# Stores of eight combined output blocks as tasks of their own, later in the order

## The chip, the cores and the metric

The kernel runs on one core of one Trainium2 chip. The metric is the device time of one execution in microseconds (us). A run has several executions; the time before is a median of three runs.

## The reference

The reference chains three parts: an attention through 32 memory slots per head, a first expert layer, and a second expert layer with four gated experts. Only the last one matters here:

```python
def _moe2_ref(x, domain_probs, w1, w2):
    p = domain_probs / (domain_probs.sum(-1, keepdims=True) + 1e-09)
    out = np.zeros((N, D), dtype=np.float32)        # N = 2304, D = 512
    for e in range(E):                              # E = 4, F = 1024
        h = np.maximum(x @ w1[e], 0.0)
        out += p[:, e:e + 1] * (h @ w2[e])
    return out.astype(np.float32)
```

The kernel writes the output transposed, as 512 rows of 2304 tokens. The tokens are four batches of 576.

## The kernel before, in words

The last layer works on units of one group of 512 hidden columns (eight groups g, two to an expert) and one batch b. Batches 0 and 1 go through all eight groups first (units 00, 01, 10, ... 71, written group then batch), then batches 2 and 3 (units 02, 03, 12, ... 73). Every product of blocks of two by two is done with seven products in place of eight, and each product in three passes of split operands. In a unit, `Up` makes the hidden blocks (product, line 894, six matmuls of 128x288 at line 899) and `Seven` multiplies them by the second weights (product, line 1051, six matmuls at line 1064): 14 products per unit, tasks D02_0 to D02_13 for group 0 and batch 2. The result of D02_n lies in one of two PSUM banks (pool ps_h, two buffers, tiles c020 to c0213) until its task F02_n (flush, line 1072) adds it to an accumulator in SBUF; in group 0 the flush is a copy on ScalarE (line 1082).

The accumulators of a batch are seven blocks of 128x2x288. Four of them (P2, P3, P4, P5) lie in one tile, acc0 for batch 0, and end as the four output blocks. The pool of these tiles has two buffers: acc2 of batch 2 takes the memory of acc0, and acc3 that of acc1. The first flush into acc2 is F02_4 and the first into acc3 is F03_2, both copies on ScalarE. Each must come after the last reader of the old tile.

When batches 0 and 1 are through their eighth group, `combine` (line 1086) turns the seven blocks into the four output blocks, with seven tensor additions per batch, tasks cb00 to cb06 and cb10 to cb16 on VectorE or GpSimd. The additions 1, 4, 5 and 6 complete an output block; right behind each of these, in the same task, SyncE issues the store of 288 KB to the output (line 1097). That is eight stores for batches 0 and 1. Batch 2 is combined at the end of the program and batch 3 is stored by another path.

All tasks stand in one list written out by hand, `ORDER`. Every engine gets its instructions in the order of that list, and so does SyncE, which issues all DMAs. SyncE issues one DMA after the other: where one waits for a semaphore, those behind it wait too. Among the DMAs around the change are loads of the next unit's weights: tasks wr (line 827, into the tiles w170 and w171 in place, piece by piece as TensorE has read the old one) and cl (line 861, into tiles w2c in a ring of seven), reloads of batch 3 (line 733), gates (line 882) and writes of derived weights to DRAM (line 820).

Of the kernel before, what the change touches and what calls it, by code (L numbers as in the profile page):

```python
# [185 lines left out]
c22_021 p1_030 v1_030 D71_10 cl00 cl02 D71_13 x3l1 cl03 F71_13 p4_021 c21_021 F71_10 sk7S1 x3h3 D02_1 H02_1 p3_021
cb06 x3h6 x3l6 p1_031 E71_11 D71_11 x3l3 F71_11 x3t2 cl01 p5_031 F02_1 cb04 D71_12 D02_0 x3t3 x3h5 c12_021 x3h4 x3l4
p5_030 p6_030 wr103 cl06 F02_0 v16_030 p2_030 c11_030 F71_12 p7_030 cb05 x3l5 wr100 v1_031 p6_031 wr113 p2_031 wr105
v167_030 p4_030 c22_030 p3_030 S02_4 H02_4 cb11 H02_2 L02_2 p5_120 D02_4 F02_4 L02_1 c12_030 v16_031 cl04 H02_3 D02_2
c21_030 D02_3 S02_5 L02_4 L02_3 p7_031 cb10 F02_3 F02_2 D02_5 D02_6 p1_120 H03_0 F02_5 v167_031 D02_7 p4_031 cl05  # L190
S02_6 wr102 H02_6 F02_7 wr106 H02_5 wr115 D02_9 F02_9 cb12 cb15 c11_031 c22_031 F02_6 v1_120 p3_031 D02_8 F02_8 L03_0
D03_1 L02_5 D02_11 L02_6 F03_1 D02_13 F02_11 D02_12 wr110 S03_1 c12_031 H03_3 wr112 F02_12 p2_120 H03_1 F02_13 D03_0
c21_031 F03_0 cb13 cb16 L03_1 L03_3 p6_120 v16_120 H03_2 wr116 L03_2 D02_10 F02_10 c11_120 cb14 S03_4 cl10 H03_4 D03_2
L03_4 F03_2 p7_120 v167_120 c22_120 D03_3 F03_3 cl11 D03_4 F03_4 S03_5 H03_5 p4_120 c21_120 H12_0 L03_5 L12_0 D03_5
F03_5 cl12 p3_120 c12_120 D03_6 F03_6 p1_121 v1_121 D03_7 F03_7 cl13 p6_121 v16_121 D03_8 F03_8 S03_6 H03_6 p5_121
p2_121 c11_121 D03_9 F03_9 cl14 p7_121 v167_121 c22_121 D03_10 F03_10 D03_11 F03_11 cl15 S12_1 H12_1 L03_6 p4_121
c21_121 H12_2 L12_2 D03_12 F03_12 L12_1 p3_121 c12_121 D03_13 F03_13 cl16 p1_130 v1_130 D12_0 F12_0 p6_130 H12_3
v16_130 pg12 D12_1 F12_1 S12_4 H12_4 L12_4 L12_3 p5_130 p2_130 c11_130 D12_2 F12_2 wr200 wr203 p7_130 v167_130 c22_130
D12_3 F12_3 D12_4 F12_4 S12_5 H12_5 p4_130 c21_130 H13_0 L12_5 L13_0 wr205 wr202 D12_5 F12_5 p3_130 c12_130 wr206
D12_6 F12_6 p1_131 v1_131 D12_7 F12_7 p6_131 v16_131 D12_8 F12_8 S12_6 H12_6 p5_131 p2_131 c11_131 D12_9 F12_9 wr210  # L200
wr213 p7_131 v167_131 c22_131 D12_10 F12_10 D12_11 F12_11 S13_1 H13_1 L12_6 p4_131 c21_131 H13_2 L13_2 wr215 wr212
D12_12 F12_12 L13_1 p3_131 c12_131 wr216 D12_13 F12_13 p1_220 v1_220 D13_0 F13_0 p6_220 H13_3 v16_220 pg13 D13_1 F13_1
cl20 S13_4 H13_4 L13_4 L13_3 p5_220 p2_220 c11_220 D13_2 F13_2 p7_220 v167_220 c22_220 D13_3 F13_3 cl21 D13_4 F13_4
S13_5 H13_5 p4_220 c21_220 H22_0 L13_5 L22_0 D13_5 F13_5 cl22 p3_220 c12_220 D13_6 F13_6 p1_221 v1_221 D13_7 F13_7
cl23 p6_221 v16_221 D13_8 F13_8 S13_6 H13_6 p5_221 p2_221 c11_221 D13_9 F13_9 cl24 p7_221 v167_221 c22_221 D13_10
F13_10 D13_11 F13_11 cl25 S22_1 H22_1 L13_6 p4_221 c21_221 H22_2 L22_2 D13_12 F13_12 L22_1 p3_221 c12_221 D13_13
F13_13 cl26 p1_230 v1_230 D22_0 F22_0 p6_230 H22_3 v16_230 D22_1 F22_1 S22_4 H22_4 L22_4 L22_3 p5_230 p2_230 c11_230
D22_2 F22_2 wr300 wr303 p7_230 v167_230 c22_230 D22_3 F22_3 D22_4 F22_4 S22_5 H22_5 p4_230 c21_230 H23_0 L22_5 L23_0
wr305 wr302 D22_5 F22_5 p3_230 c12_230 wr306 D22_6 F22_6 p1_231 v1_231 D22_7 F22_7 p6_231 v16_231 D22_8 F22_8 S22_6
H22_6 p5_231 p2_231 c11_231 D22_9 F22_9 wr310 wr313 p7_231 v167_231 c22_231 D22_10 F22_10 D22_11 F22_11 S23_1 H23_1  # L210
L22_6 p4_231 c21_231 H23_2 L23_2 wr315 wr312 D22_12 F22_12 L23_1 p3_231 c12_231 wr316 D22_13 F22_13 p1_320 v1_320
D23_0 F23_0 p6_320 H23_3 v16_320 D23_1 F23_1 cl30 S23_4 H23_4 L23_4 L23_3 p5_320 p2_320 c11_320 D23_2 F23_2 p7_320
v167_320 c22_320 D23_3 F23_3 cl31 D23_4 F23_4 S23_5 H23_5 p4_320 c21_320 H32_0 L23_5 L32_0 D23_5 F23_5 cl32 p3_320
c12_320 D23_6 F23_6 p1_321 v1_321 D23_7 F23_7 cl33 p6_321 v16_321 D23_8 F23_8 S23_6 H23_6 p5_321 p2_321 c11_321 D23_9
F23_9 cl34 p7_321 v167_321 c22_321 D23_10 F23_10 D23_11 F23_11 cl35 S32_1 H32_1 L23_6 p4_321 c21_321 H32_2 L32_2
D23_12 F23_12 L32_1 p3_321 c12_321 D23_13 F23_13 cl36 p1_330 v1_330 D32_0 F32_0 p6_330 H32_3 v16_330 pg22 D32_1 F32_1
S32_4 H32_4 L32_4 L32_3 p5_330 p2_330 c11_330 D32_2 F32_2 wr400 wr403 p7_330 v167_330 c22_330 D32_3 F32_3 D32_4 F32_4
S32_5 H32_5 p4_330 c21_330 H33_0 L32_5 L33_0 wr405 wr402 D32_5 F32_5 p3_330 c12_330 wr406 D32_6 F32_6 p1_331 v1_331
D32_7 F32_7 p6_331 v16_331 D32_8 F32_8 S32_6 H32_6 p5_331 p2_331 c11_331 D32_9 F32_9 wr410 wr413 p7_331 v167_331
c22_331 D32_10 F32_10 D32_11 F32_11 S33_1 H33_1 L32_6 p4_331 c21_331 H33_2 L33_2 wr415 wr412 D32_12 F32_12 L33_1  # L220
p3_331 c12_331 wr416 D32_13 F32_13 p1_420 v1_420 D33_0 F33_0 p6_420 H33_3 v16_420 pg23 D33_1 F33_1 cl40 S33_4 H33_4
L33_4 L33_3 p5_420 p2_420 c11_420 D33_2 F33_2 p7_420 v167_420 c22_420 D33_3 F33_3 cl41 D33_4 F33_4 S33_5 H33_5 p4_420
c21_420 H42_0 L33_5 L42_0 D33_5 F33_5 cl42 p3_420 c12_420 D33_6 F33_6 p1_421 v1_421 D33_7 F33_7 cl43 p6_421 v16_421
D33_8 F33_8 S33_6 H33_6 p5_421 p2_421 c11_421 D33_9 F33_9 cl44 p7_421 v167_421 c22_421 D33_10 F33_10 D33_11 F33_11
cl45 S42_1 H42_1 L33_6 p4_421 c21_421 H42_2 L42_2 D33_12 F33_12 L42_1 p3_421 c12_421 D33_13 F33_13 cl46 p1_430 v1_430
D42_0 F42_0 p6_430 H42_3 v16_430 D42_1 F42_1 S42_4 H42_4 L42_4 L42_3 p5_430 p2_430 c11_430 D42_2 F42_2 wr500 wr503
p7_430 v167_430 c22_430 D42_3 F42_3 D42_4 F42_4 S42_5 H42_5 p4_430 c21_430 H43_0 L42_5 L43_0 wr505 wr502 D42_5 F42_5
p3_430 c12_430 wr506 D42_6 F42_6 p1_431 v1_431 D42_7 F42_7 p6_431 v16_431 D42_8 F42_8 S42_6 H42_6 p5_431 p2_431
c11_431 D42_9 F42_9 wr510 wr513 p7_431 v167_431 c22_431 D42_10 F42_10 D42_11 F42_11 S43_1 H43_1 L42_6 p4_431 c21_431
H43_2 L43_2 wr515 wr512 D42_12 F42_12 L43_1 p3_431 c12_431 wr516 D42_13 F42_13 p1_520 v1_520 D43_0 F43_0 p6_520 H43_3  # L230
v16_520 D43_1 F43_1 cl50 S43_4 H43_4 L43_4 L43_3 p5_520 p2_520 c11_520 D43_2 F43_2 p7_520 v167_520 c22_520 D43_3 F43_3
cl51 D43_4 F43_4 S43_5 H43_5 p4_520 c21_520 H52_0 L43_5 L52_0 D43_5 F43_5 cl52 p3_520 c12_520 D43_6 F43_6 p1_521
v1_521 D43_7 F43_7 cl53 p6_521 v16_521 D43_8 F43_8 S43_6 H43_6 p5_521 p2_521 c11_521 D43_9 F43_9 cl54 p7_521 v167_521
c22_521 D43_10 F43_10 D43_11 F43_11 cl55 S52_1 H52_1 L43_6 p4_521 c21_521 H52_2 L52_2 D43_12 p1_530 L52_1 F43_12
p3_521 c12_521 D43_13 F43_13 cl56 v1_530 D52_0 F52_0 p6_530 v16_530 pg32 H52_3 S52_4 D52_1 F52_1 H52_4 L52_4 p5_530
wr603 p2_530 c11_530 D52_2 wr600 F52_2 p7_530 v167_530 c22_530 D52_3 F52_3 D52_4 S52_5 F52_4 L52_3 p4_530 c21_530
H53_0 L53_0 wr605 H52_5 L52_5 wr602 D52_5 F52_5 p1_531 p3_530 wr606 c12_530 D52_6 F52_6 D52_7 v1_531 p6_531 F52_7
D52_8 F52_8 S52_6 H52_6 L52_6 D52_9 F52_9 p5_531 wr613 v16_531 p2_531 c11_531 p7_531 v167_531 c22_531 D52_10 F52_10
S53_1 H53_1 p4_531 c21_531 H53_2 L53_2 D52_12 F52_12 D52_11 p5_620 wr612 L53_1 p3_531 wr616 p1_620 v1_620 F52_11
# [1348 lines left out]
```

## Time and profile before

| | us |
|---|---|
| median of 3 runs | 1100.35 (1099.81 to 1100.35) |
| the profiled execution | 1100.15 |
| its span, first to last instruction | 1098.4 |
| PE (TensorE matmul) busy | 1089.1 (99% of the span) |
| DVE (VectorE) busy | 804.6 |
| ACT (ScalarE) busy | 562.1 |
| POOL (GpSimd) busy | 548.3 |

The profile names engines by these short names; SP is SyncE and SPq its queue of DMA issues. A bracket [0.92 <-DMA w2c<-kS] behind a row is the time that the engine stood idle before it, and what ended the wait. The granted clock of TensorE is given as a share of its full 2.4 GHz.

### The profile page before, as it was taken

The page shows a single profiled execution, that of the slowest core. Times are in us where ns is not written, and L with a number is a line of the kernel's source. Part 1 is how long each engine was busy: PE and PEld are TensorE (multiplying, and loading weights), DVE is VectorE, ACT ScalarE, POOL GpSimd, SP SyncE. Part 2 cuts the span into 40 slices and gives each one's busy share as a digit, 9 for nine tenths or more (in the row PEclk, how much of TensorE's full clock was granted, in tenths as well). Part 3 has the DMA queues.
Part 4 walks back from the last instruction along what each step waited for, and adds up shares of the span by engine and source line. Part 5 has one row for each costly group of instructions (what it writes and reads, how often), then busy time and mean ns, then how long its engine had stood idle before and what let it go on. Part 6 is the DMA issues. An engine that isn't in the chain of part 4 may idle for free.

```text
span 1098.4 us, 22039 instructions
## 1 busy us (share of the span) xinstructions
PE 1089.1 (99%) x8550; PEld 1055.4 (96%) x8550; DVE 804.6 (73%) x1520; ACT 562.1 (51%) x1236; POOL 548.3 (50%) x443
## 2 busy tenths in 40 slices
...
GB/s 375 395 149 20 81 75 59 77 22 59 1 52 37 154 137 306 198 235 260 203 198 225 252 233 188 266 239 287 192 182 166 163 193 154 176 164 165 184 144 87
DMA packets 62584, 185.40 MB, mean 169 GB/s; under 512 B 6288, under 2 KB 24720, under 8 KB 58768
## 3 DMA queue, kind: packets, MB, share of 16 engines
...
HBM read 117.62 MB, written 66.36 MB: 167 GB/s over the span
## 4 chain that ended last, share of the span: by engine, by line
PE 96%; DVE 2%; DMA 1%; issue 0%; SPq 0%; POOL 0%; ACT 0%; DVEq 0%; POOLq 0%
PE c L1064 30%; PE y L705 18%; PE uy L899 13%; PE uw L899 9%; PE ux L899 9%; PE h L671 9%; PE y L702 1%; PE pw L630 1%; PE warm L337 1%; PE o L1010 1%; PE pm L439 1%; PE h L668 1%; DMA w2c<-kS 1%; DMA w<-kw 1%; PE pc L471 0%; DVE h L1037 0%
## 5 line engine op out<-in xcount | busy, mean ns | idle before, releaser
L324 POOL TENSOR_TENSOR gc<-h,gc 128x576 fp32r<-128x576 f32 x102 | 149.5, 1473 | 204.7 <-ACT gc L1045 204.3
L705 PE MATMUL y<-g,wout 128*128 128x288 f32 x1440 | 205.5, 296 | 0.0
L705 PEld LDWEIGHTS y<-g,wout 128*128 128x128 f32 x1440 | 195.4, 188 | 7.3 <-ACT g L690 2.5
L1045 ACT CAST gc<-h 128x576 fp32r<-128x576 f32 x217 | 142.9, 674 | 115.0 <-DVE h L1037 69.8
L1064 PE MATMUL c<-gc,w2c 128*128 128x288 f32 x1260 | 192.3, 295 | 0.9 <-DMA w2c<-kS 0.9
L1084 DVE TENSOR_TENSOR acc<-c,acc 128x288 f32<-128x288 f32 x280 | 124.2, 453 | 83.5 <-PE c L1064 83.0
L899 PE MATMUL uy<-x,w 128*128 128x288 f32 x1152 | 183.1, 295 | 0.2 <-DMA w<-kw 0.2
L1064 PEld LDWEIGHTS c<-gc,w2c 128*128 128x128 f32 x1260 | 175.3, 188 | 1.3 <-ACT gc L1045 1.1
L899 PEld LDWEIGHTS uy<-x,w 128*128 128x128 f32 x1152 | 163.0, 188 | 0.4 <-ACT v L971 0.4
L324 POOL TENSOR_TENSOR g<-act,g 128x288 fp32r<-128x288 f32 x81 | 70.3, 875 | 123.6 <-ACT g L690 92.6
L899 PE MATMUL uw<-x,w 128*128 128x288 f32 x768 | 122.9, 296 | 0.2
L899 PE MATMUL ux<-x,w 128*128 128x288 f32 x768 | 121.7, 295 | 0.0
L1064 PE MATMUL c<-gc,sS 128*128 128x288 f32 x768 | 117.8, 295 | 1.1 <-DVE acc L1084 1.1
L671 PE MATMUL h<-a,wp 128*128 128x288 f32 x720 | 110.2, 296 | 0.0
L899 PEld LDWEIGHTS uw<-x,w 128*128 128x128 f32 x768 | 108.7, 188 | 0.9 <-DVE ux L936 0.6
L899 PEld LDWEIGHTS ux<-x,w 128*128 128x128 f32 x768 | 108.7, 188 | 0.0
L324 DVE TENSOR_TENSOR gc<-h,gc 128x576 fp32r<-128x576 f32 x115 | 100.5, 883 | 10.9 <-ACT gc L1045 10.7
L1064 PEld LDWEIGHTS c<-gc,sS 128*128 128x128 f32 x768 | 106.9, 188 | 1.4 <-DVE acc L1084 1.4
L686 DVE SCALAR_TENSOR_TENSOR act<-neg,bet,h 128x288 f32<-128x288 f32 x120 | 60.3, 510 | 63.9 <-ACT neg L677 57.4
L671 PEld LDWEIGHTS h<-a,wp 128*128 128x128 f32 x720 | 99.9, 188 | 5.7 <-issue 2.3
L677 ACT ACTIVATE neg<-h 128x288 f32<-128x288 f32 x128 | 52.1, 411 | 98.0 <-PE h L671 95.5
L1082 ACT COPY acc<-c 128x288 f32<-128x288 f32 x154 | 60.3, 401 | 75.1 <-PE c L1064 74.1
...
## 6 DMA issues: line engine op xcount, KB each, us to landing
...
```

What stands on the lines that cost most here:

```text
L324: eng.tensor_tensor(out=out, in0=in0, in1=in1.bitcast(F32), op=ALU.subtract)
L337: mm(p[:, 0:128], ident, ident, start=True, stop=True)
L439: mm(p[32 * h:32 * h + 32, 0:128], l, r, start=(c == 0), stop=(c == 4))
L671: mm(p, wp_t[b, c, g][:, x, fs], a_t[b][:, y, g, o:o + HB], start=(n == 0), stop=(n == 5))
L677: nc.scalar.activation(out=self.neg, in_=self.p, func=AF.Relu, scale=-1.0)
L686: nc.vector.scalar_tensor_tensor(out=self.g, in0=self.neg, scalar=bet[:, ft:ft + 1], in1=self.p, op0=ALU.mult, op1=ALU.add)
L705: mm(First.acc[d], w[:, x, d * 128:(d + 1) * 128], self.gt[:, y, 0:HB], start=(self.start and n == 0), stop=(self.stop and n == 2))
L899: mm(p, w[:, x, a, k], operand(self.b, i)[:, y, k], start=(start and n == 0), stop=(n == 5), skip_group_check=not start)
L1045: nc.scalar.copy(out=t[:, 0], in_=self.raw(q))
L1064: mm(p, w[:, x, i, m * 128:(m + 1) * 128], self.g_t[q][:, y, i], start=(fresh and k == 0), stop=(k == 5), skip_group_check=not fresh)
L1082: nc.scalar.copy(out=a, in_=self.ps[n])
L1084: nc.vector.tensor_tensor(out=a, in0=self.ps[n], in1=a, op=ALU.add)
```

## The change

The store leaves `combine` and becomes a function of its own. For batches 0 and 1 it is a task cs, added to the plan for the additions 1, 4, 5 and 6; in `ORDER` each cs stands some 14 tasks behind its cb. Batch 2 stores as before. Only the eight cs are new in the list; the rest of it is the same, with other line breaks. Of the list the first changed line is shown, where cs01 comes in 14 tasks behind cb01.

```diff
-p1_021 S71_6 E70_13 D71_1 F71_1 E71_5 vl711 pg03 D70_13 cb00 F70_13 x3t0 p5_021 E71_3 D71_5 D71_3 v16_020 F71_5 x2h6
...
+p1_021 S71_6 E70_13 D71_1 F71_1 E71_5 vl711 pg03 D70_13 cb00 F70_13 cs01 x3t0 p5_021 E71_3 D71_5 D71_3 v16_020 F71_5
...
-        if b < 3 and o in (P2, P3, P4, P5):
+        if b == 2:
+            store(b, n)
+
+    def store(b, n):
+
+        o = (P6, P2, P7, P6, P3, P4, P5)[n]
+        a = acc_t[b]
+        if o in (P2, P3, P4, P5):
             i, j = divmod((P2, P3, P4, P5).index(o), 2)
             rows = out[i * 256:(i + 1) * 256, b * S + j * HB:b * S + (j + 1) * HB]
             nc.sync.dma_start(out=rows.rearrange("(m p) n -> p m n", p=128), in_=a[o])
...
         def do_combine(b, n):
             do(f"cb{b}{n}", combine, b, n)
+            if b < 2 and n in (1, 4, 5, 6):
+                do(f"cs{b}{n}", store, b, n)
```

No instruction is added or removed. On the compute engines no instruction changes its place. What moves is on SyncE, in three stretches; two of them follow. In these rows a name like w2c06 is a tile (down weights of group 0, product 6), the number behind it a buffer, and the brackets list the semaphores that the instruction waits for. DMAs take eight semaphores DMAHW0 to DMAHW7 in turn, and each first waits for the DMA that had its semaphore before, so a DMA's own semaphore is among those in its brackets, except where that wait is left out because it holds already.

SyncE from the second store of acc0 to the load of w2c04, before:

```order
L1097 DMA out_0<-acc0_5207 128x2x288 [waits DMAHW4_49,DVE_49]
L861 DMA w2c01_9885<-kS10_5760 128x1024 [waits DMAHW5_49,PE_49]
L1097 DMA out_0<-acc0_5207 128x2x288 [waits DMAHW6_49,DVE_49]
L827 DMA w170_8872<-kw110_5794 128x2x512 [waits DMAHW7_49,PE_49]
L861 DMA w2c06_9936<-kw2011_5830 128x1024 [waits DMAHW3_49,DMAHW0_49]
L1097 DMA out_0<-acc0_5207 128x2x288 [waits DMAHW1_49,DVE_49]
L827 DMA w170_8872<-kw110_5794 128x2x512 [waits DMAHW2_49,PE_49]
L827 DMA w171_8992<-kw111_5895 128x2x512 [waits PE_49]
L827 DMA w170_8872<-kw110_5794 128x2x256 [waits DMAHW4_49]
L1097 DMA out_0<-acc1_5524 128x2x288 [waits DMAHW5_49,Pool_49]
L861 DMA w2c04_10018<-kS30_5751 128x1024 [waits DMAHW6_49]
```

And with the change:

```order
L861 DMA w2c01_9884<-kS10_5760 128x1024 [waits DMAHW4_49,PE_49]
L1104 DMA out_0<-acc0_5207 128x2x288 [waits DMAHW5_49,DVE_49]
L827 DMA w170_8872<-kw110_5794 128x2x512 [waits DMAHW6_49,PE_49]
L861 DMA w2c06_9935<-kw2011_5830 128x1024 [waits DMAHW7_49,DMAHW3_49]
L1104 DMA out_0<-acc0_5207 128x2x288 [waits DMAHW0_49,DVE_49]
L827 DMA w170_8872<-kw110_5794 128x2x512 [waits DMAHW1_49,PE_49]
L827 DMA w171_8992<-kw111_5895 128x2x512 [waits DMAHW2_49,PE_49]
L827 DMA w170_8872<-kw110_5794 128x2x256
L1104 DMA out_0<-acc0_5207 128x2x288 [waits DMAHW4_49,DVE_49]
L861 DMA w2c04_10017<-kS30_5751 128x1024 [waits DMAHW5_49]
L1104 DMA out_0<-acc1_5524 128x2x288 [waits DMAHW6_49,Pool_49]
```

The last store of acc0 stood ahead of the three loads into w170 and w171, and stands behind them now.

SyncE from the third store of acc1 to the load of w2c11 or the last store of acc1, before and with the change:

```order
L1097 DMA out_0<-acc1_5524 128x2x288 [waits DMAHW6_49,DVE_49]
L827 DMA w171_8992<-kw111_5895 128x2x256 [waits DMAHW7_49,PE_49]
L1097 DMA out_0<-acc1_5524 128x2x288 [waits DMAHW0_49,Pool_49]
L861 DMA w2c10_10217<-kw2100_6010 128x1024 [waits DMAHW1_49,PE_49]
L861 DMA w2c11_10247<-kS11_5704 128x1024 [waits DMAHW2_49,PE_49]
```

```order
L827 DMA w171_8992<-kw111_5895 128x2x256 [waits DMAHW6_49,PE_49]
L861 DMA w2c10_10215<-kw2100_6010 128x1024 [waits DMAHW7_49,PE_49]
L1104 DMA out_0<-acc1_5524 128x2x288 [waits DMAHW0_49,DVE_49]
L861 DMA w2c11_10246<-kS11_5704 128x1024 [waits DMAHW1_49,PE_49]
L1104 DMA out_0<-acc1_5524 128x2x288 [waits DMAHW2_49,Pool_49]
```

The last store of acc1 now stands behind the load of w2c11. That load goes into the buffer of w2c01 and waits for TensorE to finish the last product that reads w2c01, which is c033.

Who waits for these stores has not moved. ScalarE around F02_4 (the copy of c024 into acc2), and TensorE at the products behind it, with the change:

```order
L1045 CAST gc0_5140<-h021_9727 128x576
L1082 COPY acc2_9893<-c024_10004 128x288 [waits DMAHW1_49,DMAHW4_49,DMAHW0_49,DMAHW5_49,DVE_49,PE_49]
L945 COPY v16031_10015<-uy031_9959 128x288 [waits DVE_49,Activation_49]
L1045 CAST gc0_5140<-h021_9727 128x576
L1082 COPY acc2_9893<-c023_10028 128x288 [waits PE_49]
```

```order
L1064 MATMUL c024_10004<-gc0_5140,w2c02_9823 128x288 x4
L1064 MATMUL c022_10020<-gc2_5260,w2c01_9884 128x288 [waits DMAHW4_49]
L1064 MATMUL c022_10020<-gc2_5260,w2c01_9884 128x288 [waits DVE_49]
L1064 MATMUL c022_10020<-gc2_5260,w2c01_9884 128x288 x4
L1064 MATMUL c023_10028<-gc2_5260,w2c01_9884 128x288 [waits Activation_49]
```

The copy waits for four DMAs, the four stores of acc0; before they are those on DMAHW7, 4, 6 and 1, with the change those on DMAHW1, 5, 0 and 4, the last of which is the third row from the end of the second list. The wait of c023 on ScalarE is for this copy, since c023 takes the PSUM bank of c024. F03_2 waits in the same way for the four stores of acc1, and c034, two products behind c032, for F03_2.

## Rows read from the trace of the kernel before

**Rows 1.** The page, first part: busy time by engine.

```profile
PE 1089.1 (99%) x8550; PEld 1055.4 (96%) x8550; DVE 804.6 (73%) x1520; ACT 562.1 (51%) x1236; POOL 548.3 (50%) x443
```

**Rows 2.** Waits of PE from 700 to 850 us: total, times, longest.

```profile
PE c L1064 <- DVE acc L1084: 1.1, 1, 1.1
PE c L1064 <- DMA w2c<-kS: 0.9, 1, 0.9
```

**Rows 3.** Waits of SyncE's queue, 715 to 780 us, same columns.

```profile
SPq L1097 <- DVE acc L1093: 21.9, 5, 7.3
...
SPq L1097 <- DVE ux L936: 1.9, 1, 1.9
```

**Rows 4.** Timeline of SyncE around the stores: start, length, DMA issued.

```profile
746.68 0.42 SPq L861 DMA_DIRECT2D w2c<-kS  x1
748.22 0.39 SPq L1097 DMA_DIRECT2D out<-acc  x1
751.88 0.53 SPq L827 DMA_DIRECT2D w<-kw  x1
752.50 0.55 SPq L861 DMA_DIRECT2D w2c<-kw  x1
754.65 0.39 SPq L1097 DMA_DIRECT2D out<-acc  x1
755.15 2.04 SPq L827 DMA_DIRECT2D w<-kw  x3
757.29 0.54 SPq L1097 DMA_DIRECT2D out<-acc  x1
757.88 0.46 SPq L861 DMA_DIRECT2D w2c<-kS  x1
...
771.60 0.38 SPq L1097 DMA_DIRECT2D out<-acc  x1
773.04 0.34 SPq L861 DMA_DIRECT2D w2c<-kw  x1
777.02 0.34 SPq L861 DMA_DIRECT2D w2c<-kS  x1
```

**Rows 5.** Issue to landing, us, of stores issued at 746.20, 748.22, 754.65, 757.29, 771.60.

```profile
out<-acc SPq DMA_DIRECT2D x1, 288.0 KB, 2.4
...
out<-acc SPq DMA_DIRECT2D x1, 288.0 KB, 4.3
...
out<-acc SPq DMA_DIRECT2D x1, 288.0 KB, 3.6
...
out<-acc SPq DMA_DIRECT2D x1, 288.0 KB, 7.0
...
out<-acc SPq DMA_DIRECT2D x1, 288.0 KB, 3.3
```

**Rows 6.** Timeline of PE: products of units 02 and 03.

```profile
757.29 2.67 PE L1064 MATMUL c<-gc,w2c 128*128 128x288 f32 x18
...
765.63 1.03 PE L1064 MATMUL c<-gc,w2c 128*128 128x288 f32 x6 [0.92 <-DMA w2c<-kS]
...
773.65 1.75 PE L1064 MATMUL c<-gc,w2c 128*128 128x288 f32 x12
775.24 0.96 PE L899 MATMUL uy<-x,w 128*128 128x288 f32 x6
776.03 1.75 PE L1064 MATMUL c<-gc,w2c 128*128 128x288 f32 x12
```

**Rows 7.** Timeline of ACT: F02_4 and F03_2.

```profile
758.43 0.40 ACT L1082 COPY acc<-c 128x288 f32<-128x288 f32 x1 [3.41 <-PE c L1064]
...
775.64 0.41 ACT L1082 COPY acc<-c 128x288 f32<-128x288 f32 x1
```

**Rows 8.** Windows: length, busy (count) of PE, clock, DMA share, GB/s (first two); all engines (last two).

```profile
1.36:5.10 3.74, 3.74 (x18) 1.00 0.84 241
5.10:8.84 3.74, 3.74 (x36) 1.00 1.06 409
...
1094.75:1096.90 2.15, 0.00 (x0) 0.00 (x0) 0.46 (x1) 0.00 (x0) 0.00 (x0) 1.00 0.74 255
...
1097.30:1097.40 0.10, 0.00 (x0) 0.00 (x0) 0.00 (x0) 0.00 (x0) 0.00 (x0) 0.50 0.00 0
```

More of the change, by code (lines that the diff above doesn't have):

```diff
@@ L186 @@
[L186 to L239, printed above, removed]
-D52_13 F52_13 wr615 c12_531 D53_0 F53_0 S53_4 H53_3 p6_620 v16_620 wr610 pg33 H53_4 D53_1 F53_1 L53_3 L53_4 S53_5
@@ L241 @@
-p2_620 p7_620 c11_620 D53_2 F53_2 v167_620 c22_620 D53_4 F53_4 D53_3 cl60 F53_3 cl61 p4_620 H53_5 L53_5 c21_620 H62_0
-L62_0 D53_5 F53_5 p3_620 c12_620 D53_6 cl64 p1_621 D53_7 F53_6 v1_621 p6_621 D53_8 F53_8 F53_7 v16_621 S53_6 H53_6
-p2_621 c11_621 D53_9 F53_9 p7_621 cl62 p5_621 v167_621 c22_621 D53_10 F53_10 S62_1 H62_1 D53_11 F53_11 p4_621 p3_621
-c12_621 c21_621 L53_6 H62_2 D53_12 F53_12 p1_630 L62_2 L62_1 D53_13 F53_13 v1_630 D62_0 H62_3 p6_630 v16_630 F62_0
-D62_1 F62_1 p5_630 S62_4 H62_4 L62_3 p2_630 c11_630 D62_2 cl65 F62_2 wr700 wr703 p7_630 D62_4 v167_630 c22_630 D62_3
@@ new lines @@
+x2h6 D71_6 wr012 H71_5 x2l6 wr015 c11_020 us310 x3h2 p7_020 vk711 F71_3 F71_6 x3l2 v1_021 v167_020 p5_020 c22_020
+D70_12 F70_12 D71_8 F71_8 H71_6 p2_021 c11_021 E71_7 x2l5 p4_020 D71_7 c21_020 cb02 F71_7 L71_5 D71_4 F71_4 H02_0
+L71_6 p3_020 us311 E71_9 E71_13 c12_020 cb03 p6_021 v16_021 x3l0 L02_0 S02_1 wr016 D71_9 F71_9 p7_021 x3t1 v167_021
+x3h1 c22_021 p1_030 v1_030 D71_10 cl00 cl02 D71_13 x3l1 cl03 F71_13 p4_021 c21_021 F71_10 sk7S1 x3h3 D02_1 H02_1
+p3_021 cb06 x3h6 x3l6 p1_031 E71_11 D71_11 x3l3 F71_11 x3t2 cl01 p5_031 F02_1 cb04 D71_12 cs06 D02_0 x3t3 x3h5 c12_021
@@ new lines @@
+x3h4 x3l4 p5_030 p6_030 wr103 cl06 F02_0 v16_030 cs04 p2_030 c11_030 F71_12 p7_030 cb05 x3l5 wr100 v1_031 p6_031 wr113
+p2_031 wr105 v167_030 p4_030 c22_030 p3_030 S02_4 H02_4 cs05 cb11 H02_2 L02_2 p5_120 D02_4 F02_4 L02_1 c12_030 v16_031
+cl04 H02_3 D02_2 c21_030 D02_3 cs11 S02_5 L02_4 L02_3 p7_031 cb10 F02_3 F02_2 D02_5 D02_6 p1_120 H03_0 F02_5 v167_031
+D02_7 p4_031 cl05 S02_6 wr102 H02_6 F02_7 wr106 H02_5 wr115 D02_9 F02_9 cb12 cb15 c11_031 c22_031 F02_6 v1_120 p3_031
+D02_8 F02_8 L03_0 D03_1 L02_5 D02_11 L02_6 F03_1 cs15 D02_13 F02_11 D02_12 wr110 S03_1 c12_031 H03_3 wr112 F02_12
@@ new lines @@
+p2_120 H03_1 F02_13 D03_0 c21_031 F03_0 cb13 cb16 L03_1 L03_3 p6_120 v16_120 H03_2 wr116 L03_2 D02_10 F02_10 c11_120
+cb14 S03_4 cl10 cs16 H03_4 D03_2 L03_4 F03_2 p7_120 v167_120 c22_120 D03_3 F03_3 cl11 D03_4 cs14 F03_4 S03_5 H03_5
+p4_120 c21_120 H12_0 L03_5 L12_0 D03_5 F03_5 cl12 p3_120 c12_120 D03_6 F03_6 p1_121 v1_121 D03_7 F03_7 cl13 p6_121
+v16_121 D03_8 F03_8 S03_6 H03_6 p5_121 p2_121 c11_121 D03_9 F03_9 cl14 p7_121 v167_121 c22_121 D03_10 F03_10 D03_11
+F03_11 cl15 S12_1 H12_1 L03_6 p4_121 c21_121 H12_2 L12_2 D03_12 F03_12 L12_1 p3_121 c12_121 D03_13 F03_13 cl16 p1_130
@@ new lines @@
+v1_130 D12_0 F12_0 p6_130 H12_3 v16_130 pg12 D12_1 F12_1 S12_4 H12_4 L12_4 L12_3 p5_130 p2_130 c11_130 D12_2 F12_2
+wr200 wr203 p7_130 v167_130 c22_130 D12_3 F12_3 D12_4 F12_4 S12_5 H12_5 p4_130 c21_130 H13_0 L12_5 L13_0 wr205 wr202
+D12_5 F12_5 p3_130 c12_130 wr206 D12_6 F12_6 p1_131 v1_131 D12_7 F12_7 p6_131 v16_131 D12_8 F12_8 S12_6 H12_6 p5_131
+p2_131 c11_131 D12_9 F12_9 wr210 wr213 p7_131 v167_131 c22_131 D12_10 F12_10 D12_11 F12_11 S13_1 H13_1 L12_6 p4_131
+c21_131 H13_2 L13_2 wr215 wr212 D12_12 F12_12 L13_1 p3_131 c12_131 wr216 D12_13 F12_13 p1_220 v1_220 D13_0 F13_0
@@ new lines @@
+p6_220 H13_3 v16_220 pg13 D13_1 F13_1 cl20 S13_4 H13_4 L13_4 L13_3 p5_220 p2_220 c11_220 D13_2 F13_2 p7_220 v167_220
+c22_220 D13_3 F13_3 cl21 D13_4 F13_4 S13_5 H13_5 p4_220 c21_220 H22_0 L13_5 L22_0 D13_5 F13_5 cl22 p3_220 c12_220
+D13_6 F13_6 p1_221 v1_221 D13_7 F13_7 cl23 p6_221 v16_221 D13_8 F13_8 S13_6 H13_6 p5_221 p2_221 c11_221 D13_9 F13_9
+cl24 p7_221 v167_221 c22_221 D13_10 F13_10 D13_11 F13_11 cl25 S22_1 H22_1 L13_6 p4_221 c21_221 H22_2 L22_2 D13_12
+F13_12 L22_1 p3_221 c12_221 D13_13 F13_13 cl26 p1_230 v1_230 D22_0 F22_0 p6_230 H22_3 v16_230 D22_1 F22_1 S22_4 H22_4
@@ new lines @@
+L22_4 L22_3 p5_230 p2_230 c11_230 D22_2 F22_2 wr300 wr303 p7_230 v167_230 c22_230 D22_3 F22_3 D22_4 F22_4 S22_5 H22_5
+p4_230 c21_230 H23_0 L22_5 L23_0 wr305 wr302 D22_5 F22_5 p3_230 c12_230 wr306 D22_6 F22_6 p1_231 v1_231 D22_7 F22_7
+p6_231 v16_231 D22_8 F22_8 S22_6 H22_6 p5_231 p2_231 c11_231 D22_9 F22_9 wr310 wr313 p7_231 v167_231 c22_231 D22_10
+F22_10 D22_11 F22_11 S23_1 H23_1 L22_6 p4_231 c21_231 H23_2 L23_2 wr315 wr312 D22_12 F22_12 L23_1 p3_231 c12_231 wr316
+D22_13 F22_13 p1_320 v1_320 D23_0 F23_0 p6_320 H23_3 v16_320 D23_1 F23_1 cl30 S23_4 H23_4 L23_4 L23_3 p5_320 p2_320
@@ new lines @@
+c11_320 D23_2 F23_2 p7_320 v167_320 c22_320 D23_3 F23_3 cl31 D23_4 F23_4 S23_5 H23_5 p4_320 c21_320 H32_0 L23_5 L32_0
+D23_5 F23_5 cl32 p3_320 c12_320 D23_6 F23_6 p1_321 v1_321 D23_7 F23_7 cl33 p6_321 v16_321 D23_8 F23_8 S23_6 H23_6
+p5_321 p2_321 c11_321 D23_9 F23_9 cl34 p7_321 v167_321 c22_321 D23_10 F23_10 D23_11 F23_11 cl35 S32_1 H32_1 L23_6
+p4_321 c21_321 H32_2 L32_2 D23_12 F23_12 L32_1 p3_321 c12_321 D23_13 F23_13 cl36 p1_330 v1_330 D32_0 F32_0 p6_330
+H32_3 v16_330 pg22 D32_1 F32_1 S32_4 H32_4 L32_4 L32_3 p5_330 p2_330 c11_330 D32_2 F32_2 wr400 wr403 p7_330 v167_330
@@ new lines @@
+c22_330 D32_3 F32_3 D32_4 F32_4 S32_5 H32_5 p4_330 c21_330 H33_0 L32_5 L33_0 wr405 wr402 D32_5 F32_5 p3_330 c12_330
+wr406 D32_6 F32_6 p1_331 v1_331 D32_7 F32_7 p6_331 v16_331 D32_8 F32_8 S32_6 H32_6 p5_331 p2_331 c11_331 D32_9 F32_9
+wr410 wr413 p7_331 v167_331 c22_331 D32_10 F32_10 D32_11 F32_11 S33_1 H33_1 L32_6 p4_331 c21_331 H33_2 L33_2 wr415
+wr412 D32_12 F32_12 L33_1 p3_331 c12_331 wr416 D32_13 F32_13 p1_420 v1_420 D33_0 F33_0 p6_420 H33_3 v16_420 pg23 D33_1
+F33_1 cl40 S33_4 H33_4 L33_4 L33_3 p5_420 p2_420 c11_420 D33_2 F33_2 p7_420 v167_420 c22_420 D33_3 F33_3 cl41 D33_4
@@ new lines @@
+F33_4 S33_5 H33_5 p4_420 c21_420 H42_0 L33_5 L42_0 D33_5 F33_5 cl42 p3_420 c12_420 D33_6 F33_6 p1_421 v1_421 D33_7
+F33_7 cl43 p6_421 v16_421 D33_8 F33_8 S33_6 H33_6 p5_421 p2_421 c11_421 D33_9 F33_9 cl44 p7_421 v167_421 c22_421
+D33_10 F33_10 D33_11 F33_11 cl45 S42_1 H42_1 L33_6 p4_421 c21_421 H42_2 L42_2 D33_12 F33_12 L42_1 p3_421 c12_421
+D33_13 F33_13 cl46 p1_430 v1_430 D42_0 F42_0 p6_430 H42_3 v16_430 D42_1 F42_1 S42_4 H42_4 L42_4 L42_3 p5_430 p2_430
+c11_430 D42_2 F42_2 wr500 wr503 p7_430 v167_430 c22_430 D42_3 F42_3 D42_4 F42_4 S42_5 H42_5 p4_430 c21_430 H43_0 L42_5
```

51 lines of the change are left out of this document (33 added, 18 removed).

## Prediction, made before the changed kernel ran

> **What bounds the kernel.** I read the page's busy times first. TensorE (PE) is busy for 1089.1 of 1098.4 us [rows 1]: whatever makes PE wait lengthens the run by about as much, and whatever shortens another engine's queue brings only what PE waits for it now. So the second view is PE's list of waits in the stretch of the change. From 700 to 850 us it has two entries, 1.1 us for an addition on DVE and 0.9 us for a load of down weights [rows 2]. The first comes at about 721 us, ahead of every store. Only the 0.9 us hang on SyncE's queue. The queue itself waits far longer: stores waited 21.9 us for combining additions, in five waits, once 7.3 us [rows 3]. The reader should see the gap between the two: the loads behind the stores are late, but PE nearly never is.
>
> The third view is the timeline of SyncE beside those of PE and ACT, for the other side of the stores: who waits until they have landed. The first flush into acc2, F02_4 on ACT, needs all four stores of acc0 landed, since acc2 lies in the memory of acc0. It starts at 758.43 [rows 7]. The last of those stores was issued at 754.65 [rows 4] and landed 3.6 us later [rows 5], at 758.25. The view of waits names PE as what ended ACT's wait [rows 7], and c024 did end then (757.29 plus 0.96, the length of six matmuls in any such row): 758.25 as well. The store had no room left. F03_2 starts at 775.64 [rows 7]; its last store was issued at 771.60 and took 3.3 us, to 774.9 [rows 4, 5]. That is 0.7 us of room. These two margins are what the change moves.
>
> **The change part by part.** No instruction is added; eight stores of 288 KB move.
>
> *What comes earlier.* A write of derived weights and the gates of batch 3, which stood behind the 7.3 us wait, go ahead of it. No engine has a wait for either, so 0. w2c01 goes ahead of its store: 0 too, since its product started at 758.1 without a wait. The load of w2c04, on which the 0.9 us wait ended at 765.63 [rows 6], was issued at 757.88 [rows 4]. Now a store of acc1 is behind it and not ahead, and SyncE no longer waits for the addition before 754.65. The three w loads can follow the store that now stands behind w2c06, at 752.50 + 0.55 + 0.05 + 0.39 + 0.06 = 753.55, as far as the last products on the old weights are through; I take the spacing of before, 2.14 us from 755.15 to 757.29 [rows 4], so they are issued by 755.69. A store of about 0.5 us and the load of w2c04 follow, at 756.2, that is 1.7 us earlier. The 0.9 us go. **Gain 0.9 us.**
>
> *The last store of acc0* is now issued at 755.7, 1.05 us later than before, but behind three loads of 1.25 MB. How long it takes there can be read from the same place: the store of acc1 that was issued at 757.29, right behind the same three loads, took 7.0 us [rows 4, 5]. Bounds: 3.6 us (the store one place earlier, behind less), so landed at 759.3; and landing at 764.3, when the old one did (757.29 + 7.0), if the transfers are limited by bytes, since the same bytes stand ahead of it. I take 7.0 us, as it is the same place in the queue: 762.7. F02_4 starts 0.15 us later, at 762.85, in place of 758.43. That is 4.4 us (1.0 to 6.0). What waits for it: c024 and c022 fill the two PSUM banks, and c023 needs the bank that F02_4 empties. Before, c023 ran at once: 18 matmuls follow each other from 757.29 [rows 6], the third product at 758.88, as F02_4 ended at 758.83. So PE has no slack and takes the whole delay. ACT's casts behind F02_4 are late by as much, as is PE; nothing more is added. **Loss 4.4 us.**
>
> *The last store of acc1* now stands behind the load of w2c11, and that load waits for the end of c033 on PE. It was issued at 777.02 [rows 4], as c033 (the first of two products from 776.03 [rows 6]) ended. But F03_2, the flush of c032, wants that store, and before ran at 775.64, while c033 was running. Now: load at 777.02, store 0.4 later, landing, 0.15, copy 0.41 [rows 7], and then c034, which needs the bank of c032. For the landing the ends are 2.4 us (a store alone) and 7.0 (in the full queue) [rows 5]. I take 4.3, the store of 748.22, which also followed a 512 KB load (746.68) on a queue otherwise at rest [rows 4, 5]. That makes 777.02 + 0.4 + 4.3 + 0.15 + 0.41 = 782.3. Before, c034 started at 776.83. **Loss 5.5 us** (3.6 to 8.2). Both losses stay in the sum, as the second is counted from the end of c033, however late that is. The other six stores land well before the one that ends each wait: 0.
>
> *TensorE's clock.* Two pauses of 4.4 and 5.5 us are longer than any that PE has here. What such a pause costs besides can be bounded. At the end of the program the last matmul ended at 1094.75; the granted clock was 1.00 until 1097.1 and 0.50, the lower level of 1.2 GHz, from 1097.3 [rows 8]: it fell some 2.5 us after the last work. At the start PE ran 18 of its first matmuls in 3.74 us and 36 of the same in the next 3.74 [rows 8]; the column reads 1.00 there, but the count is that of the lower level. So a fall costs about half of 3.74, 1.9 us, before the rate is back; no fall costs 0. I count one fall, in the longer pause. **Loss 1.9 us** (0 to 3.8). The Trainium skill (TensorE: Matmul & The Clock Gate, Part 1) says that half rate is the default and that activity releases the throttle. By that rule both pauses would be paid for, 3.8 us; the end of this trace agrees with it, at 0.50 after idling.
>
> **Sum**: 4.4 - 0.9 + 5.5 + 1.9 = 10.9 us. On the profiled execution's 1100.15 that is 1111.05; the median of the runs shown lies 0.2 higher, so 1111.2.
>
> **Rivals.**
> - *Clock falls in both pauses*: 1113.1. For: 2.5 us to the fall at the end is shorter than either. Against: it is one observation, at the end of the program.
> - *Clock falls in neither*: 1109.3.
> - *A store needs not wait for the loads ahead of it.* Then the first lands at 755.7 + 2.4 = 758.1 and costs nothing; the second costs 777.02 + 0.4 + 2.4 + 0.56 - 776.83 = 3.6, less 0.9: 2.7, with a fall of the clock 4.6, so 1103 to 1105. For: stores alone land in 2.4 us. Against: 7.0 us at that very place. The Trainium skill (DMA: Bandwidth & Descriptors, Queues, rings and completion order) says that completion is not FIFO per issuing engine, which is this rival; 7.0 against 2.4 us speaks for a queue that is served in order as far as a whole store goes.
> - *Not slower*: the late stores land before the flushes, and only the gain on w2c04 is left, 1099.4. The point from which it decides: the store of acc0 issued at 755.7 has to land by 758.25, and that of acc1, which cannot be issued before 777.4, has to land by about 776. The second can't be if F03_2 really waits for it; so this needs a copy that doesn't wait as its row says. More than 0.9 us can't come back, as PE has no more waits there.
> - *The change doesn't do what it says*: the order of SyncE's rows shows that it does. No chance of its own.
>
> **How the numbers follow.** Forecast (both waits, one fall) 0.37; both falls 0.27; no fall 0.15; not in order 0.10; not slower 0.08, with 0.02 of that for a gain that I don't see; more than 1115.5, by a second stall that I have missed, 0.03. The range from 1105.0 to 1115.5 takes in the first three with the bounds of the first store (3.4 us less, 1.6 more) and of the second (1.9 less, 2.7 more), though not all ends at once, and leaves out the last three. A measurement of this kernel can tell 0.2%, 2.2 us, from no change: faster by more 0.02, within it 0.06, slower 0.92.
>
> **What would show it.** Right: in PE's waits two new entries, for ACT's copy at line 1082, of about 4 and 5 us, some 20 us apart, at c023 and c034; ACT's waits there put down to a DMA out<-acc; the wait for w2c gone; lower clock in a stretch behind one or both; the rest of the program shifted by the sum. Wrong: PE without waits at 759 and 780 us, or waits shorter than 3 us; a loss elsewhere, such as a w load that comes late because the stores are now in front of it.

## The result, and the profile after

The changed kernel takes 1114.45 us (median of four runs, 1113.18 to 1116.23); the kernel before, beside it, 1100.35. The ratio is 1.0129, with a 95% interval from 1.0117 to 1.0141. The forecast was 1111.2, with 1105.0 to 1115.5: the side and the mechanism came out, and the time is 3.3 us over the forecast. The profiled execution took 1116.23.

The page's busy times, against [rows 1]. PE is 7.2 us busier, although it has the same 8550 matmuls: they took longer, by some 4.9 us around the stores and 2.5 near the start (below).

```profile
PE 1096.3 (98%) x8550; PEld 1061.9 (95%) x8550; DVE 805.2 (72%) x1520; ACT 562.3 (50%) x1236; POOL 547.0 (49%) x443
```

PE's waits from 700 to 850 us, against [rows 2]: total, times, longest. The load of w2c is gone from the list, and ACT's copy has come, twice.

```profile
PE c L1064 <- ACT acc L1082: 10.1, 2, 6.0
PE c L1064 <- DVE acc L1084: 1.1, 1, 1.1
```

ACT's waits in the same stretch, in the same columns. Both copies wait for a DMA that carries an accumulator to the output:

```profile
ACT acc L1082 <- DMA out<-acc: 14.7, 2, 8.0
```

The timeline of ACT shows where [rows 7]: F02_4 and F03_2, which started at 758.43 and 775.64 before.

```profile
765.56 0.40 ACT L1082 COPY acc<-c 128x288 f32<-128x288 f32 x1 [8.00 <-DMA out<-acc]
...
791.09 0.40 ACT L1082 COPY acc<-c 128x288 f32<-128x288 f32 x1 [6.74 <-DMA out<-acc]
```

The timeline of PE, against [rows 6]. The row at 766.01 is c023, the one at 791.54 is c034. Behind each wait six matmuls take 1.8 or 1.6 us where they take 0.96 elsewhere; behind the first, twelve take 3.02 in place of 1.75.

```profile
758.21 2.05 PE L899 MATMUL uw<-x,w 128*128 128x288 f32 x12
760.10 1.75 PE L1064 MATMUL c<-gc,w2c 128*128 128x288 f32 x12
766.01 1.81 PE L1064 MATMUL c<-gc,w2c 128*128 128x288 f32 x6 [4.17 <-ACT acc L1082]
767.62 1.64 PE L899 MATMUL uy<-x,w 128*128 128x288 f32 x6
769.06 3.02 PE L1064 MATMUL c<-gc,w2c 128*128 128x288 f32 x12
771.92 0.96 PE L899 MATMUL ux<-x,w 128*128 128x288 f32 x6
...
784.62 0.96 PE L1064 MATMUL c<-gc,w2c 128*128 128x288 f32 x6
791.54 1.81 PE L1064 MATMUL c<-gc,w2c 128*128 128x288 f32 x6 [5.96 <-ACT acc L1082]
793.15 1.64 PE L899 MATMUL uy<-x,w 128*128 128x288 f32 x6
794.59 1.50 PE L1064 MATMUL c<-gc,w2c 128*128 128x288 f32 x6
795.92 0.96 PE L899 MATMUL uw<-x,w 128*128 128x288 f32 x6
```

The windows of the same stretch, against [rows 8], give the reason: length, busy (count) of each engine in the order of the page, granted clock, DMA share, GB/s. Behind the first wait the clock is 0.50, and 0.81 in the next 5 us; behind the second it is 0.50 again. The last window, near the start of the program, is taken up below.

```profile
765.00:770.00 5.00, 3.99 (x16) 3.99 (x17) 3.10 (x5) 2.54 (x6) 0.00 (x0) 0.50 0.87 322
770.00:775.00 5.00, 5.00 (x33) 5.00 (x33) 3.70 (x6) 2.25 (x5) 2.22 (x2) 0.81 0.75 211
...
790.00:795.00 5.00, 3.46 (x14) 3.46 (x15) 1.10 (x3) 1.98 (x5) 0.57 (x1) 0.50 0.03 12
...
20.00:60.00 40.00, 38.21 (x414) 25.40 (x413) 34.94 (x83) 28.29 (x73) 23.59 (x23) 0.96 0.93 366
```

SyncE's timeline, against [rows 4]: the store at 758.70 is the last of acc0, that at 786.04 the last of acc1.

```profile
756.20 2.40 SPq L827 DMA_DIRECT2D w<-kw  x3
758.70 0.56 SPq L1104 DMA_DIRECT2D out<-acc  x1
759.31 0.52 SPq L861 DMA_DIRECT2D w2c<-kS  x1
759.92 0.40 SPq L1104 DMA_DIRECT2D out<-acc  x1
...
785.61 0.34 SPq L861 DMA_DIRECT2D w2c<-kS  x1
786.04 0.39 SPq L1104 DMA_DIRECT2D out<-acc  x1
```

And from issue to landing, against [rows 5], of the DMAs issued at 758.70, 759.31 and 786.04:

```profile
out<-acc SPq DMA_DIRECT2D x1, 288.0 KB, 6.7
...
w2c<-kS SPq DMA_DIRECT2D x1, 512.0 KB, 7.3
...
out<-acc SPq DMA_DIRECT2D x1, 288.0 KB, 4.8
```

758.70 + 6.7 = 765.4, and the copy starts at 765.56; 786.04 + 4.8 = 790.8, and the copy starts at 791.09.

**Where the time went.** From the start of c024 (757.29 before, 760.10 after) to the same product of unit 03 (the uw at 779.22 before, at 795.92 after) it was 21.93 us before and 35.82 after: 13.9 us more. Waits: 4.17 and 5.96 new, 0.92 gone, so 9.2. The rest is 4.7, of which slow matmuls are 4.5 (2.6 behind the first wait and 1.9 behind the second; worked out below). Another 0.28 us lies just ahead, in the twelve matmuls of uw (2.05 us; 1.77 before). In sum 14.2, beside a difference of the medians of 14.1; the runs scatter by 3 us, so the agreement is closer than they warrant.

The remaining 2.5 us by which c024 is late in the profiled execution lie near the start. The same four matmuls (line 668) start at 30.30 before and 31.39 after, the next four at 32.91 and 35.52: 1.1 us are lost ahead of the first and 1.5 more ahead of the second. From 5.10 to 8.84 us PE did 26 matmuls where it did 36 before [rows 8], and around 31 us the clock was at the lower level (PE alone: length, busy (count), clock, DMA share, GB/s):

```profile
5.10:8.84 3.74, 3.74 (x26) 1.00 1.07 411
31.20:34.60 3.40, 3.21 (x21) 0.50 1.00 417
```

That fall makes the 0.96 between 20 and 60 us (1.00 before). The change touches nothing there, and the run with late stores that has no such wait (four tiles, below) showed the same 0.96 in its profiled execution: it is a matter of the execution, not of the change. At the uw of unit 03 the profiled execution is 16.7 us late and at its end 16.1; where the 0.6 us come back was not taken apart.

### The profile page after: what moved, and what is told of

Same layout as the page of the kernel before. It is cut to its first block, busy times and chain, and to the rows that moved or that the text cites. A ratio compares the mean times of both kernels' runs of the same rounds, so it can differ in the third digit from the quotient of the medians.

```text
span 1114.4 us, 22040 instructions
## 1 busy us (share of the span) xinstructions
PE 1096.3 (98%) x8550; PEld 1061.9 (95%) x8550; DVE 805.2 (72%) x1520; ACT 562.3 (50%) x1236; POOL 547.0 (49%) x443
## 4 chain that ended last, share of the span: by engine, by line
PE 96%; DVE 2%; DMA 1%; issue 0%; ACT 0%; POOL 0%; SPq 0%; ACTq 0%; DVEq 0%; POOLq 0%
PE c L1064 31%; PE y L705 17%; PE uy L899 14%; PE ux L899 9%; PE uw L899 9%; PE h L671 9%; PE y L702 1%; PE warm L337 1%; PE pw L630 1%; PE o L1010 1%; DMA out<-acc 1%; PE pm L439 1%; PE h L668 1%; PE pc L471 0%; DVE h L1037 0%; DVE h L958 0%
## 5 line engine op out<-in xcount | busy, mean ns | idle before, releaser
L1064 PE MATMUL c<-gc,w2c 128*128 128x288 f32 x1260 | 195.9, 298 | 10.1 <-ACT acc L1082 10.1
L1064 PEld LDWEIGHTS c<-gc,w2c 128*128 128x128 f32 x1260 | 178.5, 191 | 10.7 <-ACT acc L1082 10.6
```

What stands on the lines that cost most here:

```text
L1064: mm(p, w[:, x, i, m * 128:(m + 1) * 128], self.g_t[q][:, y, i], start=(fresh and k == 0), stop=(k == 5), skip_group_check=not fresh)
```

## The experiments

The theory: the loss is two waits for memory. F02_4 and F03_2 wait for the last store of acc0 and of acc1, and the clock falls in the pauses that this gives PE. The rivals: the stores in their new places crowd or delay the weight loads; or the stores are late but something else holds the copies.

**One store back: cs05.** Only the last store of acc0 goes back to right behind its addition.

```diff
-cb05 x3l5 wr100
+cb05 cs05 x3l5 wr100
...
-H02_4 cs05 cb11
+H02_4 cb11
```

> Of the changed kernel, only the last store of acc0 (cs05) goes back to right behind its addition cb05; the other seven stay late. Theory of two waits (each of ACT's two first flushes waits for the last store of the memory that it takes over): the wait of PE at c023 falls from 4.2 us to about 1 us (one more store, cs04, now stands ahead of cs05 in the queue), the wait at c034 stays at about 6 us with its slow clock behind it; time 1108 to 1109.5 us. Rival (the loss is late weight loads, as stores and loads now share a full DMA queue): the waits at c023 and c034 both stay and the time is within 2 us of the changed kernel's 1114.5.

Measured 1108.28 us (1107.40 to 1109.39), ratio 1.0071 (1.0057 to 1.0084). PE's timeline has the wait at c034 as in the changed kernel, and 1.25 us in place of 4.17 at c023:

```profile
760.08 1.07 PE L1064 MATMUL c<-gc,w2c 128*128 128x288 f32 x6 [1.25 <-ACT acc L1082]
...
782.83 1.81 PE L1064 MATMUL c<-gc,w2c 128*128 128x288 f32 x6 [5.80 <-ACT acc L1082]
```

Matmuls are slow behind the second wait alone. At 760.08 1.25 us are left. Two stores now stand next to each other in SyncE's order, where there was one before, which would account for them; no run takes that apart.

**The other store back: cs14.** Only the last store of acc1.

```diff
-cb14 S03_4
+cb14 cs14 S03_4
...
-D03_4 cs14 F03_4
+D03_4 F03_4
```

> Only the last store of acc1 (cs14) goes back to right behind its addition cb14; the other seven stay late. Theory of two waits: c023 waits 4.2 us as in the changed kernel; at c034 about 1.8 us are left, because the third store of acc1 (cs16) still stands behind the load of w2c10; no low clock there; time 1106.5 to 1109 us. Rival (late loads): within 2 us of 1114.5.

Measured 1107.38 us (1106.99 to 1108.11), ratio 1.0063 (1.0049 to 1.0076). The mirror image:

```profile
764.26 1.81 PE L1064 MATMUL c<-gc,w2c 128*128 128x288 f32 x6 [4.36 <-ACT acc L1082]
...
784.45 1.07 PE L1064 MATMUL c<-gc,w2c 128*128 128x288 f32 x6 [1.70 <-ACT acc L1082]
```

The 1.70 us are the next late store: cs16 is now the last one of acc1. So each wait has its own store, and undoing one leaves the other's cost.

**Three stores back: cs05, cs14 and cs16.** The other five stay late.

```diff
-cb05 x3l5 wr100
+cb05 cs05 x3l5 wr100
...
-H02_4 cs05 cb11
+H02_4 cb11
...
-cb16 L03_1
+cb16 cs16 L03_1
...
-cb14 S03_4 cl10 cs16 H03_4
+cb14 cs14 S03_4 cl10 H03_4
...
-D03_4 cs14 F03_4
+D03_4 F03_4
```

> Three stores go back (cs05 of acc0; cs14 and cs16 of acc1), five stay some 14 tasks late. Theory of two waits: c034 does not wait, c023 at most 1 us, the clock stays at 1.00; w2c04 comes somewhat earlier and its 0.9 us wait shrinks: 1099.6 to 1101.5 us, so no difference from before that can be told. Rival (late loads): the five moved stores keep their share, five eighths of 14 us, some 1109 us.

Measured 1100.21 us (11 runs, 1099.72 to 1101.06), ratio 0.9999 (0.9990 to 1.0008). The whole loss is gone with three of eight stores; PE's waits on ACT are down to one:

```profile
PE c L1064 <- ACT acc L1082: 1.0, 1, 1.0
```

That 1.0 us, again at c023, stands in for the 0.9 us that the earlier w2c04 saves.

**All stores late, but nobody waits for them.** The four output blocks of a batch become four tiles in a pool of eight buffers, in place of one tile of four blocks in a pool of two: the same memory, but each first copy into a block now waits for that block's old store alone. The order is that of the changed kernel.

```diff
-("accp", "acc", 2)
+("accp", "acc", 8)
...
-                a = unit(f"acc{b}", pool=pools["acc"]).rearrange("p (c m n) -> p c m n", c=4, m=2)
-                l = [a[:, i] for i in range(4)]
+                l = [pools["acc"].tile([128, 2, HB], F32, tag="acc", name=f"accb{b}{i}") for i in range(4)]
```

> All eight stores stay as late as in the changed kernel; the four output blocks of an accumulator become four tiles of their own (same memory, eight buffers), so that a flush waits only for the store of the block whose memory it takes over. Theory of two waits: both waits of PE on ACT are gone although no DMA moved, the clock stays at 1.00, and the 0.9 us wait for w2c04 is gone too: 1099.2 to 1100.6 us, at or slightly below before. Rival (late loads, a full queue): DMAs as before, so about 1114 us.

Measured 1099.38 us (11 runs, 1098.31 to 1101.10), ratio 0.9989 (0.9980 to 0.9998). SyncE's timeline has the two stores as late as in the changed kernel, behind the same loads:

```profile
756.09 2.31 SPq L827 DMA_DIRECT2D w<-kw  x3
758.50 0.57 SPq L1103 DMA_DIRECT2D out<-accb  x1
...
778.41 0.34 SPq L861 DMA_DIRECT2D w2c<-kS  x1
778.84 0.39 SPq L1103 DMA_DIRECT2D out<-accb  x1
```

Yet of PE's waits from 700 to 850 us one is left, which was there before the change:

```profile
PE c L1064 <- DVE acc L1083: 1.1, 1, 1.1
```

So the transfers in their new places cost PE next to nothing by themselves (the uw ahead of c024 takes 2.02 us, about as with the change), and the rival of crowded loads falls. The loss hangs on the wait for memory of the whole tile. Nor does the wait for w2c04 come back.

**The kernel before with the four tiles.** To see whether that small gain is the tiles' or the late stores'.

```diff
-("accp", "acc", 2)
+("accp", "acc", 8)
...
-                l = [a[:, i] for i in range(4)]
+                l = [pools["acc"].tile([128, 2, HB], F32, tag="acc", name=f"accb{b}{i}") for i in range(4)]
```

> The kernel before, stores at once, with the four output blocks of an accumulator as four tiles. Tells whether the 0.9 us that the late stores with block tiles are below before come from the late stores or from the tiles. If from the stores (w2c04 issued earlier): 1100.3 us, the wait of 0.9 us for w2c04 still there. Rival (tiles alone): 1099.4 us and no such wait.

Measured 1100.38 us (12 runs, 1099.74 to 1103.12), ratio 1.0001 (0.9993 to 1.0009). The wait on the load is there:

```profile
765.67 1.03 PE L1064 MATMUL c<-gc,w2c 128*128 128x288 f32 x6 [1.07 <-DMA w2c<-kS]
```

The tiles alone bring nothing, the late stores alone lose 14 us, and the two together gain about the 0.9 us of the wait for w2c04 (1100.31 to 1099.38; the interval's upper end is 0.9998).

**cs05 behind one of the three loads.** As with three stores back, but cs05 right behind the first load (task wr100) of the three.

```diff
-cb05 cs05 x3l5 wr100 v1_031
+cb05 x3l5 wr100 cs05 v1_031
```

> As the kernel with three stores put back, but the last store of acc0 (cs05) goes right behind the first of the three weight loads (wr100) and not ahead of it. If the wait grows with the bytes ahead of the store: one more load of 512 KB at about 370 GB/s is 1.4 us, so PE waits 2.4 us at c023 (1.8 to 3.0) against 1.0 with no load and 4.2 with all three ahead; time 1101.5 to 1104 us, the upper end if the clock falls. Rival (a store lands late only if the queue is full for other reasons, not by its place): the wait stays at 1 us and the time at 1100.2.

Measured 1104.06 us (1103.75 to 1106.12), ratio 1.0037 (1.0022 to 1.0051). PE's wait, and the landing of that store (issued at 754.91):

```profile
762.25 1.06 PE L1064 MATMUL c<-gc,w2c 128*128 128x288 f32 x6 [2.76 <-ACT acc L1082]
```

```profile
out<-acc SPq DMA_DIRECT2D x1, 288.0 KB, 6.7
```

With three stores back the same store, issued at 754.75 with no load directly ahead, took:

```profile
out<-acc SPq DMA_DIRECT2D x1, 288.0 KB, 4.9
```

The wait lies between those with no load (1.0) and three loads (4.36, with cs14 back) ahead, and within what was expected; the time is just over the upper end, which was given for a fall of the clock, and the clock did fall. Against no load the landing took 1.8 us longer, and the wait is longer by as much. Against three loads it took about as long (6.9 there), and what shortened the wait was the earlier issue (754.91 against 756.75), not a shorter transfer.

**The price of the clock.** Extra matmuls keep PE working while it waits; their results are read by nobody.

```diff
-D02_2 c21_030
+D02_2 zf0 c21_030
...
-D03_3 F03_3
+D03_3 zf1 F03_3
...
-                self.ps[n] = ps_h.tile([128, 512], F32, tag="h", name=f"c{self.name}{n}")[:, 0:HB]
+                self.full = ps_h.tile([128, 512], F32, tag="h", name=f"c{self.name}{n}")
+                self.ps[n] = self.full[:, 0:HB]
...
+    def fill(product, n):
+        p = product.__self__.full
+        for i in range(n):
+            mm(p[:, 384:512], ident, ident, start=True, stop=True, skip_group_check=True)
+
+    task("zf0", fill, tasks["D02_2"][0], 38)
+    task("zf1", fill, tasks["D03_3"][0], 52)
```

> The changed kernel, with 38 extra matmuls of 128x128 on TensorE between c022 and c023 and 52 between c033 and c034, whose results nobody reads; they go into unused columns of a PSUM bank, so that TensorE is busy while it would wait. At about 0.104 us each they fill 3.9 and 5.4 us of the waits of 4.2 and 6.0 us. If part of the loss is the clock: the granted clock stays at 1.00 behind both waits, the copies still wait for the stores, and the time falls by the 4.6 us that the slow matmuls cost (2.6 behind the first wait, 2.0 behind the second), to 1109 to 1111 us. Rival (the waits alone make the loss, the slow matmuls are hidden by something later): 1114 us or more.

Measured 1119.67 us (1119.32 to 1119.86), ratio 1.0173 (1.0159 to 1.0186): missed. Each of these matmuls shows as two in the trace, so the filler took 8.65 and 11.77 us where the waits are 4.17 and 5.96. It overshot by 10.3 us and could not tell the rivals apart. The same again with half the filler:

```diff
-    task("zf0", fill, tasks["D02_2"][0], 38)
-    task("zf1", fill, tasks["D03_3"][0], 52)
+    task("zf0", fill, tasks["D02_2"][0], 17)
+    task("zf1", fill, tasks["D03_3"][0], 25)
```

> The clock's price alone, with the filler of the run before halved. The changed kernel plus 17 extra 128x128 fp32 matmuls between c022 and c023 and 25 between c033 and c034, into PSUM columns that nothing reads; all else, the late stores too, as in the changed kernel. Each such matmul was seen as two of 0.111 us, so they fill 34 x 0.111 = 3.8 us of the first wait (4.2) and 50 x 0.111 = 5.6 us of the second (6.0). If the stalls cost 4.2 + 6.0 us of waiting and the falls of the clock 2.6 + 2.0 us more: ACT's copies start as late as in the changed kernel (waits of some 8 and 6.7 us on the stores), PE's own waits on them shrink below 1 us each, the granted clock stays at 1.00 behind both, and the time falls by 4.6 us, to 1109.0 to 1111.0. If the slow matmuls behind the waits come from something else (late data, crowded DMA), the time stays at 1113.5 or more with the clock at 1.00.

Measured 1110.99 us (1110.24 to 1112.43), ratio 1.0092 (1.0073 to 1.0111). The filler fits into the waits, in PE's timeline:

```profile
759.99 3.96 PE L1544 MATMUL c<-ident 128*128 128x128 f32 x34
764.33 1.06 PE L1065 MATMUL c<-gc,w2c 128*128 128x288 f32 x6 [0.39 <-ACT acc L1083]
...
781.12 5.74 PE L1544 MATMUL c<-ident 128*128 128x128 f32 x50
787.10 1.07 PE L1065 MATMUL c<-gc,w2c 128*128 128x288 f32 x6 [0.24 <-ACT acc L1083]
```

ACT's copies wait for their stores as long as in the changed kernel:

```profile
ACT acc L1083 <- DMA out<-acc: 14.6, 2, 8.0
```

And the granted clock, third number from the end of a window's row, stays at 1.00 through both:

```profile
750.00:770.00 20.00, 19.59 (x151) 19.19 (x150) 12.92 (x22) 7.71 (x19) 7.78 (x5) 1.00 0.76 260
770.00:800.00 30.00, 29.76 (x233) 29.57 (x232) 13.15 (x23) 14.06 (x34) 11.34 (x8) 1.00 0.50 148
```

The stretch from c024 to the uw of unit 03 takes 31.2 us here (758.41 to 789.60), against 35.8: the waits are the same and 4.6 us of slow matmuls are gone. The medians differ by 3.5 us (1114.45 and 1110.99), somewhat less, and the time is at the upper end of what was expected. The runs of either kernel scatter by 2 to 3 us, but their ranges do not overlap. So the clock's share is shown in the trace with its size, and by the medians of four runs each only roughly.

## Why the prediction was right, and which term was too small

- **Gain 0.9, w2c04 earlier**: right. The 0.92 us wait is gone; with nobody waiting for the stores it is what is left (1099.38).
- **Last store of acc0, loss 4.4**: 4.17 on PE. The landing was read as 7.0 from the same place in the queue and came to 6.7. The reason given for it, the three loads directly ahead, is borne out only in part: one load directly ahead gave 6.7 as well, none 4.9 and 5.0 (with cs05 back). The store was issued 1.4 us ahead of c024 (758.70 and 760.10); the forecast had 1.6 (755.7 and 757.29). Putting this store back took the wait at c023 from 4.17 to 1.25.
- **Last store of acc1, loss 5.5**: 5.96 on PE. The landing taken was 4.3 and came to 4.8. The rest held: load issued when c033 ended, store right behind it, then copy, then c034.
- **The clock, loss 1.9**: this is the step that failed, the size of a term. The forecast counted one fall of the clock, "in the longer pause", and put the other at nothing. It fell in both. Behind the longer one, the second, it cost 1.9 us, as forecast (c034 to uw: 4.38 us, and 2.50 with filler); behind the first, which was left out, 2.6 (c023 to the ux at 771.92: 5.91, and 3.28 with filler). With 0.1 by which the second pause itself is shorter with filler, that is 4.6. With 4.6 in place of 1.9 the forecast's sum would be 13.6, and 1113.9. This was the rival "clock falls in both pauses", to which 0.27 were given against 0.37. The row for it was there: at the end of the program the clock had fallen 2.5 us after the last work [rows 8], and both pauses were longer. The Trainium skill (TensorE: Matmul & The Clock Gate, Part 1) calls half rate the default state, which activity releases; by that rule both pauses are paid for, and this trace agrees, with 0.50 behind both. Shorter pauses were not all paid for (last section).
- **Rival, a store need not wait for the loads ahead**: its time fell, as the landing took 6.7 us and not 2.4. In the changed kernel the four DMAs from 758.70 on also land in the order of issue (for the first two 765.4 and 766.6). Whether it is that order which makes a store late stays open (last section).
- **Rival, not slower**: fell for the change as it is, but it is what the four tiles give. The copy does wait as its row says; what can be taken away is the reason for it.
- **Not foreseen**: 0.28 us in the uw product ahead of c024. It is there with four tiles (2.02 us) and with three stores back (1.97) too, and not in the kernel before with four tiles (1.77), so it goes with the late stores or earlier loads and not with the waits; it was not taken apart.
